# A gated recurrence with a mixture of adapters: load and store buffers at the front of SBUF, rows at multiples of 256 bytes

## The chip, the core and the metric

One core of a Trainium2 chip (trn2) runs the whole kernel in one launch. The metric is the device time in microseconds (us) of that core; lower is better. The engines are named as in the profile: PE is TensorE's matmul and PEld its weight load, DVE is VectorE, ACT ScalarE, POOL GpSimd, SP SyncE, whose queue issues nearly all DMAs here.

## What is computed

Inputs `q`, `k`, `v`, `alpha` have the shape (4, 8, 768, 48), f32: batch, heads, time steps, head size. First a gated linear recurrence for each batch and head, then a mixture of two adapters out of eight on the 3072 rows of 384 values:

```python
for t in range(S):
    state = alpha[:, :, t, :, None] * state + np.einsum('bhd,bhe->bhde', k[:, :, t], v[:, :, t])
    y[:, :, t] = np.einsum('bhd,bhde->bhe', q[:, :, t], state)
# x = y with its heads side by side, (3072, 384)
logits = x @ w_gate                     # the two best of 8, softmax over them
delta[mask] += w[mask, k, None] * (x[mask] @ A[e] @ B[e])
return x + delta
```

## The kernel before

The work is cut into 24 units: 4 batches times 6 chunks of 128 time steps, each for all 8 heads. A unit has about 33 small steps, each a function of its own (lines 387 to 613): `ln` takes the logarithm of `alpha` (ACT), `cum` sums it by a matmul, `eup` and `edn` take exponentials, `kgm` and `qgm` multiply `k` and `q` by them (POOL, lines 429 and 436), `vbc` casts `v` (POOL, line 443), `tr` transposes both, `kq` copies them out of PSUM, `at` multiplies them, `msk` applies the causal mask (DVE, line 499, tile `at_sb`), `kv`, `sdm` and `qs` carry the state from chunk to chunk, `av` finishes the recurrence; `xb` to `delta` are the adapters, `fin` copies the result out of PSUM (ACT, line 608, tile `o`) and `store` sends it to memory (line 613, SP's queue).

The order on every engine is fixed before the kernel runs. `plan` (line 236) makes it from a hand-written table of costs (`STAGES`), due times (`LEAD`) and buffer rings; each engine then works strictly in that order, and so does SP's queue, on which loads and stores stand mixed.

Loads: batch 0 comes chunk by chunk (24 transfers of 196,608 bytes, line 305, two of them issued by ACT); batches 1 to 3 come as one transfer for each of `a_t`, `k_t`, `q_t`, `v_t` (12 transfers of 1,179,648 bytes, line 302), in this order within a batch. All of them land in `raw` tiles of [128, 48, 64] f32 from the pool `loads` (three buffers for each of the four names), of which only the first 48 of every 64 values are written: so each transfer is made of pieces of 192 bytes, which begin every 256 bytes in the SBUF partition. A store moves an `o` tile of 128 rows of 1,536 bytes (pool `outp`, five buffers).

```python
raw[b][i] = loads.tile([P, H * NCH, 64], F4, name=name, tag=name)
eng.dma_start(out=raw[b][i][:, :, 0:D], in_=src[b].rearrange("h (c j) d -> j (h c) d", j=C))
```

Where a tile lies: SBUF tiles are laid out pool after pool in the order in which the pools are opened (lines 270 to 277), each tile padded to a multiple of 32 bytes per partition. Four small constants of the framework end at byte 16,512; `consts` follows with 20,960 bytes, so `loads` begins at byte 37,472 of each partition, which is 96 past a multiple of 256; its twelve tiles have 12,288 bytes each (48 times 256). `outp`, the last pool, begins at byte 212,160, 192 past a multiple of 256.

Of the kernel before, what the change touches and what calls it, by code (L numbers as in the profile page):

```python
# [12 lines left out]
F2 = mybir.dt.bfloat16  # L13
# [8 lines left out]
P = 128  # L22
# [233 lines left out]
def kernel(  # L256
# [10 lines left out]
):  # L267
    nc = tc.nc

    consts = ctx.enter_context(tc.tile_pool(name="consts", bufs=1))  # L270
    loads = ctx.enter_context(tc.tile_pool(name="loads", bufs=3))
    scal = ctx.enter_context(tc.tile_pool(name="scal", bufs=2))
    vpool = ctx.enter_context(tc.tile_pool(name="vpool", bufs=3))
    trsb = ctx.enter_context(tc.tile_pool(name="trsb", bufs=3))
    atsb = ctx.enter_context(tc.tile_pool(name="atsb", bufs=2))
    moep = ctx.enter_context(tc.tile_pool(name="moep", bufs=3))
    outp = ctx.enter_context(tc.tile_pool(name="outp", bufs=5))
    PS = bass.MemoryType.PSUM
    ps_s = ctx.enter_context(tc.tile_pool(name="ps_s", bufs=1, space=PS))
    ps_at = ctx.enter_context(tc.tile_pool(name="ps_at", bufs=1, space=PS))  # L280
# [64 lines left out]
    )  # L345
    warm = consts.tile([P, 512], F2, name="warm")
    nc.vector.memset(warm, 0.0)
    ones = consts.tile([P, 2], F2, name="ones")
    nc.gpsimd.memset(ones, 1.0)
    sel = consts.tile([P, 2, HP], F2, name="sel")  # L350
    nc.vector.memset(sel, 0.0)
# [37 lines left out]
    def cum(u):  # L389
        s = st[u]  # L390
        lg = lgs[(u // G) % 2][:, u % G]
        cum = ps_s.tile([P, 512], F4, name="cum", tag="m", bufs=4)
        for _ in range(1):
            nc.tensor.matmul(cum, suf[:, :], warm[:, :], start=True, stop=True)
        nc.tensor.matmul(cum[:, 0:DM], suf[:, :], lg[:, :, 0:D], start=True, stop=True)  # L395
        nc.tensor.matmul(
            cum[:, DM:DM + H], sel.rearrange("p a b -> p (a b)"),
            gap.rearrange("p a b -> p (a b)"), start=True, stop=False,
            skip_group_check=True)
        for p in range(NP):  # L400
            nc.tensor.matmul(
                cum[:, DM + 2 * p:DM + 2 * p + 2],
                lg[:, 2 * p:2 * p + 2, :].rearrange("a b s -> a (b s)"), ones[:, :],
                start=False, stop=(p == NP - 1), skip_group_check=True)
        s["cum"] = cum

# [203 lines left out]
    def store(u):  # L610
# [3 lines left out]

    emit = dict(
        ld=ld, wcast=wcast, ln=ln, cum=cum, eup=eup, edn=edn, edec=edec, kgm=kgm, qgm=qgm, vbc=vbc,
        tr=tr, kq=kq, sdm=sdm, kv=kv, at=at, msk=msk, qs=qs, av=av, xb=xb, xt=xt, xs=xs, z=z, zc=zc,
        gmx=gmx, gdf=gdf, gex=gex, gwu=gwu, grd=grd, gzw=gzw, zt=zt, zs=zs, delta=delta, fin=fin,
# [34 lines left out]
```

## Time and profile before

| | us |
|---|---|
| median of 3 runs | 166.3 (166.27 to 166.71) |
| the profiled execution, its own time | 166.16 |
| its span, first to last instruction | 164.4 |
| mean granted clock of TensorE | 0.773 |

The span leaves out 1.8 us that the profiled execution needs around it. In the views, times are counted from the start of the span. "DMA" is the busy share of the core's 16 DMA engines, by the time that their packets took; packets of one engine can overlap, so it can pass 1. A chain entry is the work or the wait that something later had to wait for.

### The profile page before, as it was taken

The page shows a single profiled execution, that of the slowest core. Times are in us where ns is not written, and L with a number is a line of the kernel's source. Part 1 is how long each engine was busy: PE and PEld are TensorE (multiplying, and loading weights), DVE is VectorE, ACT ScalarE, POOL GpSimd, SP SyncE. Part 2 cuts the span into 40 slices and gives each one's busy share as a digit, 9 for nine tenths or more (in the row PEclk, how much of TensorE's full clock was granted, in tenths as well). Part 3 has the DMA queues.
Part 4 walks back from the last instruction along what each step waited for, and adds up shares of the span by engine and source line. Part 5 has one row for each costly group of instructions (what it writes and reads, how often), then busy time and mean ns, then how long its engine had stood idle before and what let it go on. Part 6 is the DMA issues. An engine that isn't in the chain of part 4 may idle for free.

```text
span 164.4 us, 3023 instructions
## 1 busy us (share of the span) xinstructions
PE 98.2 (60%) x1106; PEld 67.5 (41%) x1112; DVE 86.8 (53%) x221; ACT 79.5 (48%) x228; POOL 61.3 (37%) x93
## 2 busy tenths in 40 slices
PE   1258587585534084967820982856868838594741
PEld 0045355353312053744710761544646716382510
DVE  1025756767120046656870389487547795768050
ACT  3334357544581044259610772984546725354641
POOL 7162615523004193850053967114193942010000
PEclk9999999879655558597895699598765985859555
DMA  6998999999999999969997999999999402020202
GB/s 104 163 146 145 175 141 181 213 201 164 170 157 169 206 184 168 165 167 184 167 165 151 162 164 188 191 169 182 180 187 234 153 0 100 0 96 0 96 0 96
DMA packets 50718, 24.18 MB, mean 147 GB/s; under 512 B 29072, under 2 KB 50704, under 8 KB 50704
## 3 DMA queue, kind: packets, MB, share of 16 engines
q1 hardware_dynamic: 48624, 23.61, 83.4%
q10 hardware_dynamic: 2080, 0.39, 1.9%
q8 instruction: 8, 0.13, 0.4%
q14 instruction: 6, 0.05, 0.1%
HBM read 19.28 MB, written 4.72 MB: 146 GB/s over the span
## 4 chain that ended last, share of the span: by engine, by line
DMA 30%; PE 23%; DVE 11%; ACT 11%; POOL 9%; SPq 7%; issue 7%; ACTq 0%; DVEq 0%; POOLq 0%
DMA q_t<-in_q_dram 26%; SPq L302 6%; POOL qg L436 5%; DMA a_t<-in_alpha_dram 4%; PE tr L461 4%; POOL kg L429 4%; PE y L601 3%; DVE wu L573 2%; PE y L522 2%; PE xt L535 2%; DVE at_sb L499 2%; DVE zw L585 2%; ACT xb L529 2%; PE cum L395 2%; PE y L509 2%
## 5 line engine op out<-in xcount | busy, mean ns | idle before, releaser
L429 POOL TENSOR_TENSOR kg<-k_t,up 128x384 bf16<-128x384 f32 x24 | 24.0, 1000 | 37.1 <-DMA k_t<-in_k_dram 26.7
L499 DVE TENSOR_TENSOR at_sb<-at,mask 128x1024 bf16<-128x1024 f32 x24 | 29.3, 1219 | 10.1 <-PE y L522 7.1
L467 DVE COPY kq<-tr 128x1024 bf16<-128x1024 bf16 x24 | 16.5, 687 | 33.9 <-PE tr L461 33.3
L436 POOL TENSOR_TENSOR qg<-q_t,dn 128x384 bf16<-128x384 f32 x24 | 23.7, 998 | 16.6 <-DMA q_t<-in_q_dram 16.5
L415 ACT ACTIVATE dn<-cum 128x384 f32<-128x384 f32 x24 | 11.8, 492 | 27.0 <-POOL qg L436 17.1
L443 POOL CAST vb<-v_t 128x384 bf16<-128x384 f32 x24 | 11.9, 506 | 29.9 <-PE y L522 13.2
L461 PE MATMUL tr<-ident,qg 128*128 128x128 bf16 x96 | 12.8, 276 | 15.2 <-POOL qg L436 15.2
L540 ACT COPY xs<-xt 128x384 bf16<-128x384 bf16 x24 | 11.6, 482 | 10.4 <-PE xt L535 10.3
L395 PE MATMUL cum<-lg,suf 128*128 128x384 bf16 x24 | 10.7, 445 | 9.7 <-ACT lg L383 6.6
L461 PEld LDWEIGHTS <-qg 128*128 128x128 bf16 x96 | 8.9, 127 | 16.3 <-POOL qg L436 16.3
L529 ACT CAST xb<-y 128x384 bf16<-128x384 f32 x24 | 11.5, 480 | 8.4 <-PE y L522 8.2
L608 ACT COPY o<-y 128x384 f32<-128x384 f32 x24 | 11.6, 483 | 6.4 <-PE y L601 6.3
L557 DVE MAX8 mx<-zc 128x8 f32<-128x8 f32 x24 | 4.0, 166 | 18.2 <-ACT zc L552 18.0
L592 PE MATMUL zt<-ident,zw 128*128 128x128 bf16 x24 | 6.4, 265 | 12.0 <-DVE zw L585 11.8
L601 PE MATMUL y<-B_all,zs 128*128 128x384 bf16 x24 | 11.0, 458 | 3.8 <-ACT zs L597 3.8
L461 PE MATMUL tr<-ident,kg 128*128 128x128 bf16 x96 | 12.3, 267 | 1.6 <-POOL kg L429 1.3
L491 PE MATMUL at<-kq 48*128 48x128 bf16 x192 | 11.8, 257 | 2.1 <-DVE kq L467 1.4
L522 PE MATMUL y<-vb,at_sb 128*128 128x48 bf16 x192 | 10.6, 201 | 3.8 <-DVE at_sb L499 2.5
L546 PE MATMUL z<-W,xs 128*128 128x136 bf16 x72 | 10.1, 262 | 4.4 <-ACT xs L540 3.3
L535 PE MATMUL xt<-ident,xb 128*128 128x128 bf16 x72 | 10.2, 265 | 4.2 <-ACT xb L529 4.0
L448 DVE TENSOR_TENSOR sdec<-kv,dec 128x384 bf16<-128x384 f32 x20 | 11.0, 549 | 3.1 <-PE kv L481 3.1
L573 DVE SCALAR_TENSOR_TENSOR wu<-zc,mx,ex 128x8 f32<-128x8 f32 x24 | 9.3, 388 | 5.4 <-ACT ex L567 5.3
(53 smaller groups left out, 188.7 us busy)
## 6 DMA issues: line engine op xcount, KB each, us to landing
out_dram<-o SPq DMA_DIRECT2D x24, 192.0 KB, 3.7
a_t<-in_alpha_dram SPq DMA_DIRECT2D x6, 192.0 KB, 5.3
q_t<-in_q_dram SPq DMA_DIRECT2D x6, 192.0 KB, 5.5
k_t<-in_k_dram SPq DMA_DIRECT2D x5, 192.0 KB, 4.8
v_t<-in_v_dram SPq DMA_DIRECT2D x5, 192.0 KB, 4.7
k_t<-in_k_dram ACTq DMA_DIRECT2D x1, 192.0 KB, 4.7
v_t<-in_v_dram ACTq DMA_DIRECT2D x1, 192.0 KB, 6.6
W_st<-in_moe_A_dram SPq DMA_DIRECT2D x3, 64.0 KB, 4.2
```

The costliest lines, as they stand in the source:

```text
L395: nc.tensor.matmul(cum[:, 0:DM], suf[:, :], lg[:, :, 0:D], start=True, stop=True)
L429: nc.gpsimd.tensor_tensor(out=s["kg"][:, :, 0:D], in0=batches[b][1][:, c], in1=s["up"], op=ALU.mult)
L436: nc.gpsimd.tensor_tensor(out=s["qg"][:, :, 0:D], in0=batches[b][2][:, c], in1=s["dn"], op=ALU.mult)
L443: nc.gpsimd.tensor_copy(out=s["vb"], in_=batches[b][3][:, c])
L461: nc.tensor.transpose(t[:, w, p, :], pair(src, p), ident[:, :])
L467: nc.vector.tensor_copy(out=s["kq"], in_=s["tr"])
L499: nc.vector.tensor_tensor(out=s["at_sb"].rearrange("p a b t -> p (a b) t"), in0=s["at"].rearrange("p a b t -> p (a b) t"), in1=_bc_mid(mas ...
L522: nc.tensor.matmul(s["y"][:, h * D:(h + 1) * D], s["at_sb"][:, hh, p, :], s["vb"][:, h, :], start=(c == 0 and h == 0), stop=False, skip_gr ...
L529: nc.scalar.copy(s["xb"], s["y"])
L535: nc.tensor.transpose(s["xt"][:, i, :], s["xb"][:, i * P:(i + 1) * P], ident[:, :])
L573: nc.vector.scalar_tensor_tensor(out=s["wu"], in0=s["zc"][:, E * R:NW], scalar=s["mx"][:, 1:2], in1=s["ex"], op0=ALU.is_ge, op1=ALU.mult, ...
L601: nc.tensor.matmul(s["y"], s["zs"][:, :], B_all[:, :], start=False, stop=True, skip_group_check=True)
```

## The change

Three pools change places: `loads` and `outp` are opened before `consts`, and a new pool `head` in front of them holds only the tile `ones`, which grows from 2 to 64 columns of bf16 (128 bytes per partition). The matmul that reads `ones` still reads its first two columns. Nothing else in the program changes; the order on the engines is made from the same tables.

```diff
+    head = ctx.enter_context(tc.tile_pool(name="head", bufs=1))
+    loads = ctx.enter_context(tc.tile_pool(name="loads", bufs=3))
+    outp = ctx.enter_context(tc.tile_pool(name="outp", bufs=5))
     consts = ctx.enter_context(tc.tile_pool(name="consts", bufs=1))
-    loads = ctx.enter_context(tc.tile_pool(name="loads", bufs=3))
...
-    outp = ctx.enter_context(tc.tile_pool(name="outp", bufs=5))
...
-    ones = consts.tile([P, 2], F2, name="ones")
+    ones = head.tile([P, 64], F2, name="ones")
...
-                lg[:, 2 * p:2 * p + 2, :].rearrange("a b s -> a (b s)"), ones[:, :],
+                lg[:, 2 * p:2 * p + 2, :].rearrange("a b s -> a (b s)"), ones[:, 0:2],
```

## Rows read from the trace of the kernel before

**Rows 1.** The page's second part: 40 slices of the span.

```profile
DMA  6998999999999999969997999999999402020202
GB/s 104 163 146 145 175 141 181 213 201 164 170 157 169 206 184 168 165 167 184 167 165 151 162 164 188 191 169 182 180 187 234 153 0 100 0 96 0 96 0 96
```

**Rows 2.** The page's first part: busy time of each engine, share, instructions.

```profile
PE 98.2 (60%) x1106; PEld 67.5 (41%) x1112; DVE 86.8 (53%) x221; ACT 79.5 (48%) x228; POOL 61.3 (37%) x93
```

**Rows 3.** The page's fourth part: the chain that ended last, by engine.

```profile
DMA 30%; PE 23%; DVE 11%; ACT 11%; POOL 9%; SPq 7%; issue 7%; ACTq 0%; DVEq 0%; POOLq 0%
```

**Rows 4.** The waits: who waited for whom, us in total, times, longest.

```profile
POOL kg L429 <- DMA k_t<-in_k_dram: 26.7, 4, 12.4
POOL qg L436 <- DMA q_t<-in_q_dram: 16.5, 4, 4.7
POOL vb L443 <- DMA v_t<-in_v_dram: 11.7, 5, 3.4
ACT lg L383 <- DMA a_t<-in_alpha_dram: 5.2, 3, 2.2
```

**Rows 5.** Windows: us, busy of each engine, granted clock, DMA share, GB/s.

```profile
core 0: us, PE busy (x) PEld busy (x) DVE busy (x) ACT busy (x) POOL busy (x), PEclk, DMA share, GB/s
18.00:20.00 2.00, 1.21 (x17) 0.91 (x15) 1.22 (x3) 0.85 (x3) 1.66 (x2) 1.00 1.53 163
121.00:125.00 4.00, 3.27 (x29) 2.03 (x27) 3.64 (x8) 2.52 (x10) 3.46 (x4) 0.50 1.11 163
112.00:112.50 0.50, 0.01 (x1) 0.00 (x0) 0.50 (x1) 0.46 (x1) 0.50 (x1) 1.00 1.03 289
```

**Rows 6.** DMA packets of three of these stretches: 18:20, 121:125, 112:112.5, in this order.

```profile
DMA packets 1722, 0.33 MB, mean 163 GB/s; under 512 B 1722, under 2 KB 1722, under 8 KB 1722
...
DMA packets 848, 0.65 MB, mean 163 GB/s; under 512 B 1, under 2 KB 848, under 8 KB 848
...
DMA packets 188, 0.14 MB, mean 289 GB/s; under 512 B 0, under 2 KB 188, under 8 KB 188
```

**Rows 7.** The stores alone, 145 to 164.4 us: q1's packets, MB, share.

```profile
q1 hardware_dynamic: 864, 1.18, 16.8%
```

**Rows 8.** Timeline of SP's queue (start, length of the issue): end of batch 0, batch 1.

```profile
27.94 1.02 SPq L613 DMA_DIRECT2D out_dram<-o  x1
...
32.39 0.83 SPq L302 DMA_DIRECT2D a_t<-in_alpha_dram  x1
33.67 6.89 SPq L302 DMA_DIRECT2D k_t<-in_k_dram  x1
41.01 6.59 SPq L302 DMA_DIRECT2D q_t<-in_q_dram  x1
47.70 7.52 SPq L613 DMA_DIRECT2D out_dram<-o  x2
55.43 0.71 SPq L302 DMA_DIRECT2D v_t<-in_v_dram  x1
```

**Rows 9.** Timeline of POOL: the first work on `q_t` and on the later `v_t`.

```profile
7.40 0.99 POOL L436 TENSOR_TENSOR qg<-q_t,dn 128x384 bf16<-128x384 f32 x1 [3.35 <-DMA q_t<-in_q_dram]
...
57.11 2.91 POOL L436 TENSOR_TENSOR qg<-q_t,dn 128x384 bf16<-128x384 f32 x3 [4.49 <-DMA q_t<-in_q_dram]
...
127.28 0.50 POOL L443 CAST vb<-v_t 128x384 bf16<-128x384 f32 x1 [2.82 <-DMA v_t<-in_v_dram]
```

**Rows 10.** Timeline of DVE: the masks of the seventh and of the last unit.

```profile
61.15 1.22 DVE L499 TENSOR_TENSOR at_sb<-at,mask 128x1024 bf16<-128x1024 f32 x1
...
149.25 1.22 DVE L499 TENSOR_TENSOR at_sb<-at,mask 128x1024 bf16<-128x1024 f32 x1
```

**Rows 11.** Timeline of ACT: first and last of the last ten copies into `o`.

```profile
124.26 0.48 ACT L608 COPY o<-y 128x384 f32<-128x384 f32 x1 [0.48 <-PE y L601]
...
161.14 0.48 ACT L608 COPY o<-y 128x384 f32<-128x384 f32 x1 [0.59 <-PE y L601]
```

**Rows 12.** The lines 349 and 436: count, ns min/median/max, first and last start.

```profile
L349 POOL MEMSET ones<- x1: 99/99/99, 1.3 to 1.3; 128x2 bf16 x1
...
L436 POOL TENSOR_TENSOR qg<-q_t,dn x24: 992/997/1002, 7.4 to 131.5; 128x384 bf16<-128x384 f32 x24
```

## The prediction, made before the change was run

> **What bounds the kernel now.** I read the slices first. The DMA engines are 90% busy or more in nearly every slice up to about 127 us, and then only the stores are left [rows 1]. No engine comes near that: PE is busy for 60% of the span, DVE for 53% [rows 2]. The chain that ended last has its largest share, 30%, in DMA [rows 3], and the waits say where: POOL waits 26.7 us for `k_t`, 16.5 for `q_t` and 11.7 for `v_t` [rows 4]. So up to 127 us the kernel follows its loads, and the last 37 us (from the first use of the last `v_t` at 127.28 [rows 9] to 164.4) follow the engines.
>
> What bounds the loads? Two stretches that hold loads alone answer it. Between 18 and 20 us the small transfers of batch 0 run, between 121 and 125 us a large one. Both move 163 GB/s [rows 5], although the first is cut into 1722 packets for 0.33 MB and the second into 848 for 0.65 MB [rows 6]. Packets of about 192 bytes and of about 768 bytes give the same rate, so the limit does not count packets; it counts bytes or the 192-byte pieces, which both have. At 163 GB/s a DMA engine moves one piece in 192 x 16 / 163 = 18.8 ns. In half a microsecond after a pause, 188 packets of the large kind went at 289 GB/s, 10.6 ns for a piece [rows 5, 6]: memory can deliver these pieces faster than the steady rate, for as long as something between can take them in. That looks like a brake on the writing side, in SBUF, that is felt once a buffer is full. And on the writing side every piece of before lies badly: it begins 96 past a multiple of 256 and ends at 288, so each one crosses a 256-byte boundary. After the change each lies within one.
>
> **The placement itself.** Constants of the framework end at 16,512, `head` adds 128: 16,640 is 65 times 256. Load tiles have 48 x 256 bytes, `o` tiles 6 x 256. So every piece and every `o` row does begin at a multiple of 256; a rival in which the placement fails has under 1 in 100 and is counted with "nothing happens".
>
> **What costs nothing.** The memset of `ones` takes 99 ns for 2 columns [rows 12]; it may take longer for 64 columns, but POOL stands idle for 3.35 us a little later, waiting for the first `q_t` [rows 9], and swallows it. Without that cover it would be some 0.1 us. The matmul reads the same two columns. No instruction is added, and no queue gets another order. `consts`, `scal` and the other tiles move too; that costs an engine nothing that a row here shows, and is bounded under the rivals.
>
> **The loads, step by step.** A large load takes 1,179,648 bytes / 163 GB/s = 7.24 us today. The ends for its time after the change: 7.24 us if nothing changes; 4.08 us at the 289 GB/s of the burst. I take 4.08, since that burst is the nearest row for these same pieces when writing does not hold them up; a crossing gone (one piece of writing where there were two) would by simple halving give 3.6, so 4.08 is not the most hopeful value.
>
> The page "DMA: Bandwidth & Descriptors" of the Trainium skill (How a descriptor splits into AXI transactions) says that a transfer is split at 256-byte boundaries, and that a read that starts off such a boundary still pays for the bytes below its start. It states this for reading; applied to our writes it would be an estimate of 9 beats against 6 for a piece, 4.8 us for a large load, and the sum below would end near 135.5.
>
> *Batch 0.* 24 small loads at 163 GB/s are 29 us, and the first large load is issued at 32.39 us [rows 8]. At 289 GB/s the 29 us would be 16.3, at most 12.7 less. But SP's queue has the stores of the first two units among the last of these loads, the first at 27.94 us [rows 8], and the units themselves need their chain of steps. I take 5 us: the first large load is issued at 27.4. Ends: 0 and 12.7.
>
> *Batch 1.* From the issue of `a_t` at 32.39 to POOL's first work on `q_t` at 57.11 [rows 8, 9] are 24.7 us: three loads of 7.24 and 3.0 of latency. After: 3 x 4.08 + 3.0 = 15.2, so `q_t` is there at 42.6. The mask of the seventh unit came 4.0 us later (61.15 [rows 10]); after, at 46.7.
>
> *The engines' pace from there.* With the loads ahead, the engines set the pace. The last ten copies into `o` run from 124.26 to 161.14 [rows 11], nine steps of 4.10 us, almost all of it when no load is left to wait for. DVE's busy time over 24 units, 86.8 / 24 = 3.6 us [rows 2], is a floor for one unit. From the seventh to the last mask there are 17 steps: 17 x 4.10 = 69.7, the last mask starts at 116.4. From the last mask to the end are 164.4 - 149.25 = 15.15 us [rows 10]. Span: 131.5 us; with the 1.8 around it, 133.3 for the profiled execution. The median of before is 0.1 above its profiled execution, which I leave out: **133**.
>
> *Do the loads stay ahead?* A batch is four loads and six stores. Five stores and a little take 16.8% of 19.4 us, 3.3 us, in 864 packets [rows 7]; six stores at 128 packets are 768, some 2.9 us. So a batch costs 4 x 4.08 + 2.9 = 19.2 us of DMA time, against 6 x 4.10 = 24.6 of the engines. Stores stand between the loads on SP's queue (two ahead of `v_t` of batch 1 [rows 8]), and wait for copies into `o`, which come earlier too. The loads stop being ahead at 4L + 2.9 = 24.6, L = 5.4 us, 218 GB/s: any gain beyond a quarter of the load time is worth no more in batches 2 and 3, since the engines are late next. At L = 5.4 the head saves about 3 us in place of 5 and batch 1 adds 4: the sum is then 139.
>
> **The rivals.** *A, the brake is at the crossing and goes* (above): 132 (L = 3.6) to 139 (L = 5.4); with a pace between 3.8 and 4.6 us a unit (17 steps: 5 us less or 8.5 more), 124 to 143.
>
> *B, the loads gain something, but less than a quarter.* Memory addresses do not change: there the pieces begin at multiples of 192, and half of them cross a 256-byte boundary on the reading side. If reading is close behind as a limit, loads remain the bound. Three batches of 4L + 2.9 in place of 31.9, and a smaller head: 22 us less and a head 3 us shorter give some 141 at L = 5.4; 155 at L = 6.4, rising to 166 at 7.24. For it: the burst lasted only half a microsecond. Against it: 289 GB/s is far from 163.
>
> *C, nothing happens.* The piece is slow because it is short. Both shapes of loads go at 163 GB/s and have nothing in common but the 192-byte piece [rows 5, 6]; all of them lie alike in SBUF, so no row of before shows a piece that lies well. Then the loads stay at 7.24 us and the time at 166.3. The Trainium skill's page "DMA: Bandwidth & Descriptors" (Specifications) puts the least transfer for the line rate at 512 bytes, and does not speak of where it starts; by that rule alone the change gives nothing, and the steady rate agrees with it as well as with mine.
>
> *D, slower.* All rows now begin at the same place in their 256 bytes, and POOL reads the load tiles while other loads land. If landing rows and POOL's reads came into each other's way, POOL's multiplies would stretch. POOL is 9% of the chain, 14.8 us [rows 3]: stretched by a tenth they cost 1.5 us, 167.8; it decides from some 3.5% on, and only if the loads gain nothing. Against it: the 24 multiplies take 992 to 1002 ns [rows 12], with the DMA engines full as well as in the quiet stretch at the end.
>
> **The numbers.** A measurement of this kernel can tell about 0.3%, 0.5 us, from no change. A has 0.55, B 0.10, C 0.26, D 0.09. Faster is A and B, 0.65; the same is C, 0.26; slower is D, 0.09. The likeliest is A at 133 us, by itself between 124 and 143. A range that holds 8 in 10 must reach C at 166.3: 124 to 167, which leaves out most of D and a few hundredths below A.
>
> **What would show it.** Right: a stretch of loads alone moves well over 218 GB/s; an issue of a large load on SP takes less than 5 us, not 6.6 to 6.9; POOL's waits for `k_t`, `q_t`, `v_t` (55 us together) shrink to a few; the seventh mask is near 47 us; the copies into `o` keep about 4.1 us from then on; the slices no longer show DMA at 9 throughout. Wrong: 163 GB/s again in a stretch of loads alone (C); a rate between 163 and 218 with DMA still at 9 up to the last `v_t` (B); multiplies of POOL above 1030 ns (D). And if the loads are fast and the time is still near 150, then it is my pace that fails: the engines wait for each other in the fixed order, and 4.1 us a unit was that of the quiet end alone.

## The result, and the profile after

The changed kernel takes **140.73 us**, before 166.29 (medians of 4 runs each): ratio 0.846, 95% interval 0.842 to 0.849. The prediction was 133, between 124 and 167. The profiled execution took 140.68 us, its span is 139.0. In the changed kernel the lines from 349 on stand one line lower than before (the mask is on line 500, POOL's multiplies on 430 and 437).

The page of the changed kernel, its parts 1, 2 (DMA share and GB/s in 40 slices) and 4 (chain by engine):

```profile
PE 95.7 (69%) x1112; PEld 65.4 (47%) x1112; DVE 86.2 (62%) x221; ACT 79.0 (57%) x228; POOL 61.6 (44%) x93
...
DMA  4998969998989889399979497797210110110202
GB/s 88 256 164 179 193 138 209 233 241 237 253 232 310 239 246 306 98 272 279 251 222 297 147 312 212 214 289 250 79 57 2 57 61 0 57 57 23 90 22 92
...
PE 44%; DVE 27%; ACT 16%; issue 5%; DMA 3%; POOL 1%; SPq 1%; ACTq 0%; DVEq 0%
```

The engines do the same work as in [rows 2], within some 3%, in a span that is 25 us shorter. DMA has fallen from 30% of the chain [rows 3] to 3%, and the slices have gaps. Two stretches of the changed kernel with loads alone, one of small loads and one of large ones (windows: us, busy of each engine, granted clock, DMA share, GB/s), and their packets:

```profile
3.00:6.00 3.00, 1.04 (x7) 0.38 (x7) 0.00 (x0) 1.71 (x4) 1.28 (x6) 1.00 1.28 259
68.00:70.00 2.00, 1.43 (x25) 1.07 (x21) 1.87 (x7) 0.98 (x4) 1.20 (x2) 1.00 1.07 320
```

```profile
DMA packets 4113, 0.78 MB, mean 259 GB/s; under 512 B 4113, under 2 KB 4113, under 8 KB 4113
...
DMA packets 834, 0.64 MB, mean 320 GB/s; under 512 B 0, under 2 KB 834, under 8 KB 834
```

Both answer to the 163 GB/s of [rows 5]. At 320 GB/s an engine needs 192 x 16 / 320 = 9.6 ns for a row, where it needed 18.8: half. At that rate a large load takes 3.7 us in place of 7.24. What is left of the waits of [rows 4]:

```profile
POOL vb L444 <- DMA v_t<-in_v_dram: 5.0, 2, 2.6
ACT lg L384 <- DMA a_t<-in_alpha_dram: 1.6, 3, 0.6
POOL kg L430 <- DMA k_t<-in_k_dram: 1.3, 1, 1.3
POOL qg L437 <- DMA q_t<-in_q_dram: 0.6, 1, 0.6
```

Together 8.5 us instead of 60. SP's queue at the change from batch 0 to batch 1, to be laid beside [rows 8], and the masks of the sixth, seventh and last unit on DVE, beside [rows 10]:

```profile
27.80 0.83 SPq L303 DMA_DIRECT2D a_t<-in_alpha_dram  x1
29.07 5.03 SPq L303 DMA_DIRECT2D k_t<-in_k_dram  x1
34.54 4.29 SPq L303 DMA_DIRECT2D q_t<-in_q_dram  x1
```

```profile
39.98 1.22 DVE L500 TENSOR_TENSOR at_sb<-at,mask 128x1024 bf16<-128x1024 f32 x1
54.02 1.22 DVE L500 TENSOR_TENSOR at_sb<-at,mask 128x1024 bf16<-128x1024 f32 x1
...
123.91 1.22 DVE L500 TENSOR_TENSOR at_sb<-at,mask 128x1024 bf16<-128x1024 f32 x1
```

The first large load goes out 4.6 us earlier than before, the seventh mask comes 7.1 us earlier, and from there on no wait for a load is longer than 0.6 us: 17 steps in 69.9 us, 4.11 each, and 15.1 us from the last mask to the end. The sixth mask, though, comes no earlier. Before, it came here:

```profile
40.23 1.22 DVE L499 TENSOR_TENSOR at_sb<-at,mask 128x1024 bf16<-128x1024 f32 x1
```

### The profile page after: what moved, and what is told of

The parts are those of the page before. It is cut to its first block, busy times and chain, and to the rows that moved or that the text cites. A ratio compares the mean times of both kernels' runs of the same rounds, so it can differ in the third digit from the quotient of the medians.

```text
span 139.0 us, 3029 instructions
## 1 busy us (share of the span) xinstructions
PE 95.7 (69%) x1112; PEld 65.4 (47%) x1112; DVE 86.2 (62%) x221; ACT 79.0 (57%) x228; POOL 61.6 (44%) x93
## 4 chain that ended last, share of the span: by engine, by line
PE 44%; DVE 27%; ACT 16%; issue 5%; DMA 3%; POOL 1%; SPq 1%; ACTq 0%; DVEq 0%
PE tr L462 7%; DVE at_sb L500 6%; PE y L602 5%; DVE zw L586 5%; DVE df L563 4%; PE cum L395 4%; PE at L492 4%; PE y L523 4%; PE z L547 4%; DVE sdec L449 4%; DVE wu L574 4%; DMA a_t<-in_alpha_dram 3%; PE y L510 3%; PE xt L536 3%; PE cum L396 3%
## 5 line engine op out<-in xcount | busy, mean ns | idle before, releaser
L444 POOL CAST vb<-v_t 128x384 bf16<-128x384 f32 x24 | 11.9, 508 | 29.1 <-PE y L523 18.8
L416 ACT ACTIVATE dn<-cum 128x384 f32<-128x384 f32 x24 | 11.8, 493 | 10.7 <-PE cum L402 10.2
L492 PE MATMUL at<-kq 48*128 48x128 bf16 x192 | 11.9, 257 | 3.5 <-DVE at_sb L500 2.1
L395 PE MATMUL cum<-warm,suf 128*128 128x512 bf16 x24 | 12.5, 522 | 1.7 <-POOL suf L343 1.4
L602 PE MATMUL y<-B_all,zs 128*128 128x384 bf16 x24 | 10.5, 436 | 3.6 <-ACT zs L598 3.6
L411 ACT ACTIVATE up<-cum 128x384 f32<-128x384 f32 x24 | 12.0, 501 | 0.0
L462 PE MATMUL tr<-ident,qg 128*128 128x128 bf16 x96 | 11.9, 262 | 0.1
L462 PE MATMUL tr<-ident,kg 128*128 128x128 bf16 x96 | 11.6, 258 | 0.0
```

The source lines that it names most:

```text
L462: nc.tensor.transpose(t[:, w, p, :], pair(src, p), ident[:, :])
L492: nc.tensor.matmul(t[:, hh, p, :], s["kq"][rows, 0, p, :], s["kq"][rows, 1, p, :], start=True, stop=True)
L602: nc.tensor.matmul(s["y"], s["zs"][:, :], B_all[:, :], start=False, stop=True, skip_group_check=True)
```

## Experiments: what it is about the place of a row

Three theories could stand behind the doubled rate. **Theory 1**: a row that crosses a 256-byte boundary is written in two goes. **Theory 2**: a row that doesn't begin at a multiple of 64 bytes is slow. **Theory 3**: the order of the tiles matters, not the place of the rows. Three kernels move everything from the load buffers on by a few bytes, by the width of `ones` alone:

```diff
-    ones = head.tile([P, 64], F2, name="ones")
+    ones = head.tile([P, 112], F2, name="ones")   # e1: rows at 96 to 288
+    ones = head.tile([P, 80], F2, name="ones")    # e2: rows at 32 to 224
+    ones = head.tile([P, 128], F2, name="ones")   # e3: rows at 128 to 320
```

**e1, by 96 bytes.**

> The changed kernel with every tile from the load buffers on moved up by 96 bytes, so that load rows occupy bytes 96 to 288 past a multiple of 256, as before the change, while the pools keep their new order. Theory 1 (a 192-byte row that crosses a 256-byte boundary is written in two goes): the loads fall back to 163 GB/s in a stretch of loads alone, time 166 us. Theory 2 (rows that do not begin at a multiple of 64 bytes are slow to write): the same, 166 us. Theory 3 (the gain comes from another order of the tiles, not from where rows begin): loads near 320 GB/s, 141 us.

Measured: 166.64 us, ratio to the kernel before 1.000 (0.996 to 1.005). Small loads alone, in the window that [rows 5] show for before:

```profile
18.00:20.00 2.00, 1.26 (x17) 0.96 (x15) 1.21 (x3) 0.85 (x3) 1.70 (x2) 1.00 1.52 166
```

The whole gain is gone, with the pools in their new order. Theory 3 falls.

**e2, by 32 bytes.**

> Moved up by 32 bytes: load rows occupy bytes 32 to 224 past a multiple of 256. They cross no 256-byte boundary, and they do not begin at a multiple of 64. Theory 1 (crossing): nothing lost, 316 to 323 GB/s and 140.7 us. Theory 2 (64-byte start): 163 GB/s and 166 us.

Measured: 141.19 us, ratio 0.849 (0.842 to 0.856), as the changed kernel. Large loads alone:

```profile
64.00:66.00 2.00, 2.00 (x23) 1.66 (x21) 1.66 (x2) 1.69 (x4) 1.85 (x3) 0.50 1.06 316
```

Rows that begin at an odd multiple of 32 are as fast as aligned ones, so long as they stay within their 256 bytes. Theory 2 falls.

**e3, by 128 bytes.**

> Moved up by 128 bytes: load rows begin at a multiple of 64 (128), and cross a 256-byte boundary (128 to 320). Theory 1 (crossing): 163 GB/s, 166 us. Theory 2 (64-byte start): 320 GB/s, 141 us.

Measured: 166.44 us, ratio 1.001 (0.997 to 1.005). Small loads alone:

```profile
18.00:20.00 2.00, 1.31 (x16) 0.94 (x14) 1.35 (x3) 0.85 (x3) 1.85 (x2) 1.00 1.53 163
```

A row that begins at 128 and ends at 320 is as slow as one from 96 to 288: it's the crossing, and in SBUF, since the data in memory lies the same in all these kernels. Where in the row the boundary falls (after 128 or after 160 bytes) makes no difference.

**e6, rows without gaps**, to count crossings:

```diff
-            raw[b][i] = loads.tile([P, H * NCH, 64], F4, name=name, tag=name)
+            raw[b][i] = loads.tile([P, H * NCH, D], F4, name=name, tag=name)
```

> The changed kernel with load rows that follow each other without a gap, every 192 bytes from a multiple of 256 on, so that of four rows two cross a 256-byte boundary (those at 192 and at 128) and two don't. Theory 1 (each crossing costs one more writing of the same length): mean of 18.8 and 9.6 ns a row, 14.2 ns, 216 GB/s in a stretch of loads alone, a large load 5.4 us, time 143 to 150 us. Rival (one bad row holds up its neighbours, or only what the packet holds counts): 163 GB/s and 166 us, or 320 GB/s and 141 us.

Measured: 144.87 us, ratio 0.868 (0.862 to 0.874). Two stretches of large loads alone:

```profile
69.00:70.00 1.00, 0.50 (x4) 0.39 (x6) 1.00 (x2) 0.56 (x2) 0.76 (x1) 1.00 1.10 217
...
81.00:82.00 1.00, 0.98 (x25) 0.90 (x22) 1.00 (x3) 0.65 (x2) 1.00 (x3) 1.00 1.10 219
```

216 GB/s was expected from half crossing and half not, and 217 and 219 came. So the mean is that of rows which pay each for itself: 9.6 ns where a row stays within 256 bytes, 18.8 where it crosses. Theory 1 holds with all, none and half of the rows crossing. The runs show the doubled time; that it is two goes at the memory is how theory 1 reads it.

**e4 and e5, loads and stores apart.** A filler tile between the two pools sets the second one off the boundary: in e4 the loads, by 96 bytes,

```diff
     head = ctx.enter_context(tc.tile_pool(name="head", bufs=1))
-    loads = ctx.enter_context(tc.tile_pool(name="loads", bufs=3))
     outp = ctx.enter_context(tc.tile_pool(name="outp", bufs=5))
+    pad = ctx.enter_context(tc.tile_pool(name="pad", bufs=1))
+    loads = ctx.enter_context(tc.tile_pool(name="loads", bufs=3))
...
+    nc.gpsimd.memset(pad.tile([P, 48], F2, name="fill"), 0.0)
```

and in e5 the stores, by 192 bytes:

```diff
     loads = ctx.enter_context(tc.tile_pool(name="loads", bufs=3))
+    pad = ctx.enter_context(tc.tile_pool(name="pad", bufs=1))
     outp = ctx.enter_context(tc.tile_pool(name="outp", bufs=5))
...
+    nc.gpsimd.memset(pad.tile([P, 96], F2, name="fill"), 0.0)
```

> Store buffers at multiples of 256, load rows at 96 past a multiple of 256, both pools still in front of the constants; one more small memset. If the gain is all in the loads: 166 us, loads 163 GB/s. If the stores bring a part of it: the part shows here, each us of store time saved on the DMA engines up to 127 us being one us of the span; 24 stores of some 0.55 us, 18 of them in that stretch, give at most 10 us, 156 us.

Measured: 166.29 us, ratio 0.995 (0.991 to 1.000), 163 GB/s:

```profile
18.00:20.00 2.00, 1.28 (x17) 0.95 (x14) 1.33 (x3) 0.85 (x3) 1.86 (x2) 1.00 1.54 163
```

> Load buffers as in the changed kernel, store buffers at 192 past a multiple of 256 as they were before the change. If the stores' place matters nothing: 140.7 us, and a store's DMA time unchanged. If it matters: at most 24 x 0.1 us of DMA time, which the engines now cover: 140.7 to 141.5 us.

Measured: 139.84 us, ratio 0.838 (0.832 to 0.844). Its interval overlaps that of the changed kernel. By e4 the place of the store buffers brings about half a per cent, at most 0.9, and with fast loads nothing that shows: so nearly all of the gain is the loads'. If theory 1 held for the reading of a store's 1,536-byte rows too, which no run here shows, there would be little to gain: seven goes in place of six, not two in place of one.

## Experiments: why 141 us and not 133

The sum had the seventh mask at 46.7 us, and it came at 54.0. **Theory F**: the place of its steps in the fixed order, made for slower loads, holds it back, and another order would win these 7 us. **Theory G**: the engines with their waits for each other fill the time, and what is won at one place is lost at another. First, what the loads still cost.

**e10, the large loads left out.**

```diff
         name, src = SRC[i]
+        if b > 0:
+            raw[b][i], batches[b][i] = raw[0][i], batches[0][i]
+            return
```

> The changed kernel without its twelve large loads: batches 1 to 3 compute on batch 0's buffers, everything else as it is, in the same order. It asks what the large loads still cost at 320 GB/s. Theory G (from the first unit on the engines and their fixed order set the end, loads no longer do): 138 to 141 us, the seventh mask still at 53 to 54 us. Rival L (loads still hold units up, at the change from batch 0 to batch 1 above all): the seventh mask near 47 us and 131 to 135 us, which is what the prediction's sum gave.

Measured: 140.49 us, ratio 0.845 (0.839 to 0.852). Its seventh and last masks:

```profile
51.22 1.22 DVE L503 TENSOR_TENSOR at_sb<-at,mask 128x1024 bf16<-128x1024 f32 x1
...
121.97 1.23 DVE L503 TENSOR_TENSOR at_sb<-at,mask 128x1024 bf16<-128x1024 f32 x1
```

With no large load at all the seventh mask comes 2.8 us earlier than in the changed kernel, not 7, and the median is the same within a few tenths. Even of these 2.8 us most need not be the loads': in e5, whose loads are those of the changed kernel, it came at 51.92. Rival L falls for this order: at 320 GB/s the large loads cost it next to nothing, and the engines in their fixed order set the time. What stands in the way shows in the changed kernel's trace, on POOL and on PE:

```profile
47.56 2.00 POOL L437 TENSOR_TENSOR qg<-q_t,dn 128x384 bf16<-128x384 f32 x2
```

```profile
48.76 0.29 PE L593 MATMUL zt<-ident,zw 128*128 128x128 bf16 x1 [3.44 <-DVE zw L586]
...
50.62 0.59 PE L462 MATMUL tr<-ident,kg 128*128 128x128 bf16 x4
```

POOL has done `qg` of the seventh unit by 48.6, but PE transposes it only at 50.62: the adapter steps of the sixth unit (`zt` and what follows it) and a cumulative sum of a later unit stand ahead of it there, and `zt` waits for DVE.

**e7 and e8, four steps of the seventh unit moved up.** In the changed kernel ACT takes the logarithm of the seventh unit only behind the copy `xb` of the sixth:

```profile
41.86 0.48 ACT L530 CAST xb<-y 128x384 bf16<-128x384 f32 x1 [2.06 <-PE y L523]
42.23 0.85 ACT L387 ACTIVATE lg<-a_t 128x768 bf16<-128x768 f32 x1
```

```diff
     order = plan()[1]
+    block = [("ln", 6), ("cum", 6), ("edn", 6), ("eup", 6)]
+    order = [n for n in order if n not in block]
+    at = order.index(("xb", 5))    # e7;  e8: ("xb", 4)
+    order[at:at] = block
```

> The changed kernel with the logarithm, the cumulative sum and the two exponentials of the seventh unit moved up on their engines, to just ahead of the copy of the sixth unit's result on ACT (41.86 us). Theory F (the seventh unit is held by its place in the fixed order, behind the end of batch 0): the seventh mask, at 54.0 us, comes about 2 us earlier, and the time falls by about as much, to 138 to 139 us. Rival G (the engines have no slack there, work only changes places): 140 to 141 us, last mask unmoved.

Measured: 141.99 us, ratio 0.853 (0.849 to 0.857). The logarithm starts at 38.35 and `kg` of the seventh unit at 42.58 in place of 45.21, but its `qg` at 47.26 in place of 47.56, behind `kg` of the eighth unit. The seventh mask comes at 53.71, 0.3 us earlier and not 2.

> The same four steps moved up further, to ahead of the copy of the fifth unit's result on ACT (36.07 us). Theory F: the seventh mask 4 to 6 us earlier than 54.0, time 135 to 137 us. Rival G: 140 to 141 us. Rival H (alpha of batch 1 has not landed by then, so ACT waits for it with batch 0's steps behind): a wait of the logarithm for a DMA appears, time above 141 us.

Measured: 142.95 us, ratio 0.857 (0.850 to 0.864). ACT and POOL in e8 (timelines; in brackets the idle time before, and what ended it):

```profile
36.32 0.84 ACT L391 ACTIVATE lg<-a_t 128x768 bf16<-128x768 f32 x1 [1.27 <-DMA a_t<-in_alpha_dram]
```

```profile
41.47 1.02 POOL L434 TENSOR_TENSOR kg<-k_t,up 128x384 bf16<-128x384 f32 x1 [4.41 <-DMA k_t<-in_k_dram]
48.15 1.00 POOL L434 TENSOR_TENSOR kg<-k_t,up 128x384 bf16<-128x384 f32 x1 [5.66 <-issue]
49.11 1.99 POOL L441 TENSOR_TENSOR qg<-q_t,dn 128x384 bf16<-128x384 f32 x2
```

The logarithm is 5.9 us earlier, and waits 1.3 us for `alpha`: rival H is seen. `kg` of the seventh unit waits 4.4 us for `k_t` and is done by 42.5. But on POOL `kg` of the eighth unit stands ahead of `qg` of the seventh, and its exponential (ACT, 47.51) is ready only at 48: `qg` of the seventh starts at 49.11, and the seventh mask comes at 55.56, 1.5 us later than in the changed kernel. The steps that I moved were not the only ones held. Theory F in this small form falls: moving four steps makes the kernel no faster.

**e9, e11 and e12, planned anew.** The table's costs of the loads are changed, so that `plan` makes another order:

```diff
-        t = 1060 if c is not None else 4500
+        t = 800 if c is not None else 3700     # e9
+        t = 800 if c is not None else 4500     # e11
+        t = 900 if c is not None else 3700     # e12
```

> The changed kernel with two numbers of its planner's table set to the faster loads (800 in place of 1060 for a small load, 3700 in place of 4500 for a large one), so that the order on all engines is made anew. Theory F: the seventh unit's steps come ahead of the end of batch 0, seventh mask 3 to 6 us earlier, 135 to 139 us. Rival G: 140 to 142 us, since the due times are as they were and the order elsewhere becomes worse by as much.

Measured: 143.05 us, ratio 0.862 (0.855 to 0.869). Its seventh and last masks:

```profile
48.41 1.23 DVE L500 TENSOR_TENSOR at_sb<-at,mask 128x1024 bf16<-128x1024 f32 x1 [0.17 <-PE at L492]
...
125.43 1.22 DVE L500 TENSOR_TENSOR at_sb<-at,mask 128x1024 bf16<-128x1024 f32 x1
```

The seventh mask is 5.6 us earlier, as theory F had it, and the 17 steps to the last take 77.0 us in place of 69.9: what one stretch gained the next lost, as theory G had it. The median is 2.3 us above that of the changed kernel, and the intervals of the two ratios don't overlap: this order is some 2% slower.

> The changed kernel with one number of its planner's table altered: 800 in place of 1060 for a small load, large loads as they were. Batch 0 is planned tighter, the rest hopefully as it was. Theory F (the place of the steps in the fixed order holds the engines back in batch 0): seventh mask near 48 us, 135 to 138 us. Theory G (what one stretch gains another loses, since the engines' work with its waits fills the time): 139 to 143 us.

Measured: **138.31 us**, ratio 0.826 (0.818 to 0.833). Its masks:

```profile
48.16 1.21 DVE L500 TENSOR_TENSOR at_sb<-at,mask 128x1024 bf16<-128x1024 f32 x1
...
121.58 1.22 DVE L500 TENSOR_TENSOR at_sb<-at,mask 128x1024 bf16<-128x1024 f32 x1
```

The seventh mask is 5.9 us earlier, the 17 steps take 73.4 us: 2.3 us remain of the 5.9. This kernel beats both others. Against the changed kernel the intervals of the two ratios don't overlap; the gain is about 2%. The time lies between what theories F and G expected.

The trace of e11 says more than the theories did. Its sixth mask comes at 32.48, 7.5 us earlier than in the changed kernel, by the order alone. Then POOL waits for loads again, first for those of batch 1, then for `q_t` of batch 2; below them the changed kernel's work on that `q_t`:

```profile
39.52 1.95 POOL L430 TENSOR_TENSOR kg<-k_t,up 128x384 bf16<-128x384 f32 x2 [8.62 <-DMA k_t<-in_k_dram]
44.12 2.90 POOL L437 TENSOR_TENSOR qg<-q_t,dn 128x384 bf16<-128x384 f32 x3 [2.64 <-DMA q_t<-in_q_dram]
...
67.25 2.91 POOL L437 TENSOR_TENSOR qg<-q_t,dn 128x384 bf16<-128x384 f32 x3 [3.22 <-DMA q_t<-in_q_dram]
```

```profile
67.24 1.96 POOL L437 TENSOR_TENSOR qg<-q_t,dn 128x384 bf16<-128x384 f32 x2 [0.60 <-DMA q_t<-in_q_dram]
```

The seventh mask of e11 comes 4.0 us after 44.12, and its thirteenth, at 71.29, 4.0 us after 67.25. From the seventh to the thirteenth mask e11 needs 23.1 us and the changed kernel 19.7; from there to the last, 50.3 and 50.2. So what e11 lost of its 5.9 us lies where POOL waits 3.2 us for a `q_t` that lands at the same time in both kernels. Rival L, which e10 ruled out for the order of the changed kernel, is back in this one. No run leaves the large loads out of e11's order, so this is read from the traces and not tested.

> As the replanned kernel, but 900 for a small load and 3700 for a large one. Theory F: 135 to 138 us; theory G: 139 to 143 us.

Measured: 146.83 us with runs from 142.86 to 148.27 and no interval: no sign that it is better than the changed kernel; more can't be said.

## Why the prediction was right, and where it was not

- **The loads bound the kernel, and crossings bound the loads: right.** Equal rates for two packet shapes had pointed at the 192-byte row [rows 5, 6]; e1, e2, e3 and e6, which change only where things lie in SBUF, show that it is the crossing on the writing side. The time alone would not have shown it: the range, 124 to 167, was wide enough to hold "nothing happens", and rival B's sum at L = 5.4 gives 141 as well. It is the rate, 320 GB/s, that decides for A.
- **The size of it: too small.** I took 4.08 us for a large load, by the burst of 289 GB/s, and called 3.6 the hopeful end, by halving. It was 3.7. The row of the burst was a bound, and the mechanism itself gave the better number. The Trainium skill's split into 256-byte transactions ("DMA: Bandwidth & Descriptors", How a descriptor splits into AXI transactions), which counts bytes fetched below the start for reads, would have given, as an estimate, 9 beats against 6, 4.8 us; the runs show two against one, so the count of transactions agrees and the count of beats doesn't.
- **Rival C, short rows are slow wherever they lie: wrong.** Rows of 192 bytes go at 320 GB/s. The least transfer of 512 bytes (the Trainium skill, "DMA: Bandwidth & Descriptors", Specifications) did not set the rate of before: with rows of the same length it went from 163 to 320.
- **Batch 0: right, on a rough guess.** First large load at 27.4 forecast, 27.80 measured.
- **Batch 1: the step that failed.** "After: 3 x 4.08 + 3.0 = 15.2, so `q_t` is there at 42.6", and the seventh mask 4.0 us later, at 46.7. The mask came at 54.02, 7.3 us late; that is all of the difference between 133.3 and the 140.68 of the profiled execution. `q_t` itself landed at 44.7 (issued at 34.54, 10.2 us to landing), 2.1 us late. POOL does not wait for it any more: it begins with it at 47.56, 2.9 us after it landed, and the mask follows 6.5 us later, not 4.0. The step took the wait that stood there before as the one that would stand there after, and so put the engines' own time at the change of batch at nothing. That time is large in the old order: from the sixth mask to the seventh the changed kernel needs 14.0 us, and e10, without large loads, 13.5 (37.73 to 51.22). Where another order has the engines ready, in e9 and e11, the step holds: `q_t` is taken at 44.12, and the mask follows 4.3 and 4.0 us later. The sixth mask of the kernel before, at 40.23, would not have shown this by itself, since one step of 4.10 from there is 44.3; the place of the seventh unit's steps in the fixed order, behind the sixth unit's adapters, had to be read too. I had asked whether the loads stay ahead in batches 2 and 3, and not whether the engines are ready at batch 1.
- **The pace: right for this order, in part by luck.** 17 steps of 4.10, 69.7 us forecast, 69.9 measured; from the last mask 15.15 and 15.1. But the six steps to the thirteenth mask (73.69) took 3.28 us each and the eleven after it 4.57: 4.10 is their mean and the pace of neither. In other orders the 17 steps take 72.1 us (e7), 77.0 (e9) and 73.4 (e11), so the 4.10 taken from the quiet end was not a property of the engines. In e11 the 3.5 us more lie at the wait for `q_t` of batch 2; of e9's 7.1 us, 3.9 lie before the thirteenth mask, where POOL waits 2.1 us for `q_t` and 2.7 for `v_t`. The rest of e9's and all of e7's stays open.
- **What costs nothing: right.** The memset of `ones` took 152 ns in place of 99, under cover. **Rival D** did not come: the median of POOL's multiplies of `q_t` is 998 ns, against 997 [rows 12].
- **Smaller slips, without weight for the result.** The 864 packets and 1.18 MB of [rows 7] are six stores (6 x 196,608 bytes), not five and a little, so six stores cost 3.3 us and not 2.9, and L = 5.4 becomes 5.3. Rival A's 124 to 143 does not follow from its parts: 132 less 5 is 127, and 139 and 8.5 more are 147.5. And of the signs named, the issue of `k_t` took 5.03 us, not less than 5.

## What to carry to other kernels

Where DMA rows are shorter than 256 bytes, as the 192-byte rows here, look at the SBUF byte at which they begin: place the pool, and choose the step from row to row, so that no row crosses a multiple of 256. Here that doubled the rate of the large loads without an instruction changed. When a bound goes, ask of the first stage behind it whether the engines would be ready before the data came: the time at which they get there in their order without the data is the floor, 51 to 54 us for the seventh mask here. A fixed order that was planned with the old cost of a load is worth planning anew once the cost changes, but has to be measured: in e11 the engines were ready earlier, and then waited for the next load.

## What was not expected of the hardware

Before, small and large loads ran at the same 163 GB/s. Without crossings they part: 259 GB/s in packets of 192 bytes, 320 in packets of 768 (first fences after the change), 11.9 and 9.6 ns for a row. The stretch of small loads has two queues at work, SP's and ACT's, but from 6 to 7 us, with SP's alone, it is 247 GB/s. So it looks as if the price of a crossing had hidden a price of the packet; no run changes the packet alone. And a row may begin 32 bytes past a boundary without any cost (316 GB/s in e2), though the title of the change asks for multiples of 256.
